# Spreading the loads of later token tiles and of output weights over the chunks of a fused attention and FFN kernel

## The chip, the cores and the metric

The kernel runs on one core of a Trainium2 chip. Its time is the device time of one execution in microseconds (us); each kernel was run several times, and the median is quoted. Three kinds of engine matter here: TensorE (PE in the profile; 8298 matmuls in the kernel before) multiplies matrices, VectorE (DVE, 1272 instructions) and ScalarE (ACT, 524) work on its results, and 16 DMA engines move data between memory and the on-chip buffer (212.49 MB). Nearly all transfers are issued by the sync engine (SP), in program order, from one queue (235,888 of 235,997 packets).

## The reference, cut to what matters

One token block of 2048 rows of 1024 goes through a layer norm with modulation, attention of 32 query heads over a window of 512 cached keys, an output projection with a gate, a second modulated layer norm and a SwiGLU FFN:

```python
h = _layernorm(x) * (1 + ca) + sa
x = x + ga * _A_ref(h, A_k_cache, A_v_cache, A_wq, A_wo)   # q = h @ wq; softmax(q k^T) v; @ wo
h = _layernorm(x) * (1 + cb) + sb
x = x + gb * _B_ref(h, B_w_gate, B_w_up, B_w_down)
```

No arithmetic changes. Only the moments change at which two kinds of load are issued.

## The kernel before

The 2048 rows are four chunks of four token tiles (128 rows, 256 KB each). A chunk's attention is a loop over 32 heads of about 3.3 us each (in the trace before 3.33 us in chunk 1, and from 3.23 us in chunk 3 to 3.69 us in chunk 0), followed by its output projection; after the four chunks come the four FFN chunks.

Query projections use a scheme with 7 products where 8 would be needed, so the query weights (1 MB for a group of four heads) also need weight sums. VectorE forms the sums during chunk 0, and the sums of each group are stored to memory (1 MB) and read back in later chunks (1 MB per group). The kernel keeps only two slots for groups of query weights, so a group's load waits until TensorE has finished with the group two before it:

```python
def load_wq(gi):                 # 2 x 512 KB, two slots
    ...
# in the head loop, i = running head
if i % 4 == 3 and i > 3:
    load_wq((i + 1) // 4 + 2)    # g computed first in the kernel
...
for k in range(4):               # chunk 0 and the groups up to HG + 1: the weight sums
    g = (i + 7 - k) // 4
    if i % 4 == (k + 1) % 4 and (3 if k < 2 else 2) <= g < HG + 2:
        weight_sums(g, DVE, V, (k,))
if i % 4 == 2 and i >= 6 and (i + 2) // 4 < HG + 2:
    store_sums((i + 2) // 4)
```

A group loaded at head 11 is thus read by VectorE at the end of head 13. The loads that the change moves stand in the same queue:

```python
if ch == 0:
    if h < 12:
        load_x(TPC + h)               # 12 token tiles at heads 0 to 11
    if h in (8, 10, 12):
        load_wo((h - 8) // 2)         # three output-weight tiles, 1 MB each

def oproj(ch, first, each):           # output projection of a chunk, 8 weight tiles through 3 slots
    ...
    for b_ in range(2, HG - 2):
        ...
        load_wo(ch * HG + b_ + 3)     # waits until TensorE is done with the slot
    for k in range(TPC * HALF):
        ...
    load_wo(ch * HG + HG + 1)         # the next chunk's second and third tile:
    load_wo(ch * HG + HG + 2)         # wait until the projection is over
```

Each head's result is also turned by a DMA transpose in the same queue (`oturn`), and layer norm tiles likewise (`ln_turn`).

The softmax here doesn't subtract the row's maximum and nothing guards it: scores larger than these inputs give would overflow.

## Time and profile before

| | before |
|---|---|
| median of 3 runs, us | 1269.97 (1269.24 to 1270.16) |
| span of the profiled run, us | 1266.0 |
| TensorE busy, us | 1246.4 (98%) |
| TensorE's waits of the table, 24 us to the end | 7.5 us |

The first view is the table of TensorE's waits from 24 us on (after the opening): who waited for whom, total us, number of waits, longest. L602 is the addition that finishes a query block, on VectorE.

```profile
PE ps L265 <- DVE arena L602: 4.0, 1, 4.0
PE ps L265 <- ACT arena L765: 1.2, 4, 0.3
PE ps L265 <- DMA arena<-wq_sums: 0.9, 1, 0.9
...
```

Two of the three have a load behind them: the 0.9 us openly, the 4.0 us through VectorE. Here is VectorE's and TensorE's timeline where the 4.0 us end (start us, us, engine, line, operation; in brackets the idle time before it and what ended it). L541 forms weight sums from the query weights.

```profile
81.61 0.69 DVE L541 TENSOR_TENSOR arena<-arena 128x1024 f16<-128x1024 bf16 x1 [4.06 <-DMA arena<-in_A_wq_dram]
82.22 0.42 DVE L602 TENSOR_TENSOR arena<-ps,arena 128x256 bf16<-128x256 f32 x1
...
82.70 1.57 PE L265 MATMUL ps<-arena 128*128 128x256 bf16 x9 [4.00 <-DVE arena L602]
```

In VectorE's order of work the addition stands behind the sums that wait for query weights, so they hold it back, and with it TensorE. The sync queue's timeline shows what stood before that load, which is the line L299 (L275 are token tiles, L503 output weights, L552 the store of sums, L676 and L371 transposes):

```profile
66.89 0.56 SPq L275 DMA_DIRECT2D arena<-in_A_x_dram  x1
67.50 0.42 SPq L503 DMA_DIRECT2D arena<-in_A_wo_dram  x1
68.03 1.82 SPq L676 DMA_TRANSPOSE arena<-arena  x1
69.89 0.57 SPq L552 DMA_DIRECT2D wq_sums<-arena  x1
70.51 0.44 SPq L275 DMA_DIRECT2D arena<-in_A_x_dram  x1
71.04 1.29 SPq L676 DMA_TRANSPOSE arena<-arena  x1
72.43 1.16 SPq L299 DMA_DIRECT2D arena<-in_A_wq_dram  x2
73.64 1.44 SPq L503 DMA_DIRECT2D arena<-in_A_wo_dram  x1
```

Issued at 72.43 us, used at 81.61 us. Last, stretches of 2 us after the wait: length, busy time of each engine with its number of instructions (TensorE, TensorE's weight loads, VectorE, ScalarE, GpSimd), the granted TensorE clock (1.00 is full), the DMA engines' share and GB/s.

```profile
80.00:82.00 2.00, 0.00 (x0) 0.00 (x0) 0.39 (x1) 0.00 (x0) 0.00 (x0) 0.93 1.09 370
82.00:84.00 2.00, 1.30 (x9) 1.05 (x10) 0.80 (x3) 1.24 (x2) 0.00 (x0) 0.50 1.07 357
84.00:86.00 2.00, 2.00 (x18) 1.81 (x17) 0.73 (x3) 0.06 (x1) 0.00 (x0) 0.50 1.74 275
86.00:88.00 2.00, 2.00 (x9) 1.11 (x8) 1.73 (x4) 0.38 (x1) 0.00 (x0) 0.50 0.96 107
88.00:90.00 2.00, 2.00 (x24) 1.50 (x22) 0.46 (x2) 1.94 (x2) 0.00 (x0) 0.87 0.89 323
```

In two of them TensorE counts as fully busy with the clock granted at half. Its matmuls of 129 columns start 108 ns apart in that time, and 57 ns apart from 89 us on. This loss is in nobody's wait.

### The profile page before, as it was taken

To read this page: it belongs to the slowest core of one execution; us is meant where nothing else is said; L and a number is where in the kernel's file an instruction comes from. 1 tells how busy PE (TensorE), PEld (TensorE's weight loads), DVE (VectorE), ACT (ScalarE), POOL (GpSimd) and SP (SyncE) were. 2 spreads that over 40 slices of the span, in tenths; PEclk is the share of its full clock that TensorE was granted. 3 is DMA by queue.
4 is the path that set the end of the run, shared out by engine and by line. 5 is a ranking of instruction groups with operands and counts; after the bars stand their busy time and mean duration, and the time that the engine had idled before them with its cause. 6 is when DMAs were issued, how large, how long until landed. Compare 5 with 4: busy or idle time off the path is not lost.

```text
span 1266.0 us, 20347 instructions
## 1 busy us (share of the span) xinstructions
PE 1246.4 (98%) x8298; PEld 711.2 (56%) x8298; DVE 613.5 (48%) x1272; ACT 379.2 (30%) x524; POOL 20.0 (2%) x41
## 2 busy tenths in 40 slices
PE   7989999999999999999999999999999999999999
PEld 4667646787457774588744444444444444444444
DVE  4968507886068770476504553245422643234321
ACT  4657404675036660267600111011100111011100
POOL 1000000000000000000000000000000000000000
PEclk9989999999999999999999999999999999999999
DMA  9997747996569874579257974037520655024200
GB/s 305 278 304 183 229 135 233 282 226 195 166 176 272 215 193 149 171 207 245 46 188 240 324 216 133 25 83 191 167 75 25 158 167 173 18 84 133 67 9 25
DMA packets 235997, 212.49 MB, mean 168 GB/s; under 512 B 106880, under 2 KB 206080, under 8 KB 232064
## 3 DMA queue, kind: packets, MB, share of 16 engines
q1 hardware_dynamic: 235888, 211.19, 59.0%
q8 instruction: 65, 1.06, 0.4%
q14 instruction: 28, 0.23, 0.1%
q10 hardware_dynamic: 16, 0.00, 0.0%
HBM read 174.07 MB, written 12.58 MB: 147 GB/s over the span
## 4 chain that ended last, share of the span: by engine, by line
PE 94%; DMA 2%; SPq 1%; DVE 1%; issue 1%; ACT 0%; DVEq 0%
PE ps L265 94%; DMA arena<-wq_sums 1%; DMA arena<-in_w_mod_dram 1%; DMA arena<-in_A_wq_dram 1%; SPq L284 1%; SPq L676 0%; DVE arena L670 0%; DVE arena L602 0%; DVE arena L748 0%; ACT arena L765 0%; DMA arena<-arena 0%; DVE arena L636 0%; SPq L275 0%; DVE arena L669 0%; DVE arena L541 0%
## 5 line engine op out<-in xcount | busy, mean ns | idle before, releaser
L265 PE MATMUL ps<-arena 128*128 128x512 bf16 (+4 forms) x8249 | 1243.1, 313 | 13.3 <-DMA arena<-in_w_mod_dram 4.3
L265 PEld LDWEIGHTS ps<-arena 128*128 128x128 bf16 (+1 forms) x8249 | 708.0, 98 | 547.8 <-issue 10.9
L653 ACT ACTIVATE arena<-ps 128x1024 bf16<-128x1024 f32 x256 | 249.7, 1022 | 40.3 <-PE ps L265 37.3
L977 ACT ACTIVATE arena<-ps 128x512 bf16<-128x512 f32 x112 | 66.9, 597 | 518.0 <-PE ps L265 518.0
L680 DVE TENSOR_TENSOR arena<-ps,arena 128x512 bf16<-128x512 f32 (+1 forms) x65 | 44.4, 684 | 338.9 <-PE ps L265 338.9
L978 DVE SCALAR_TENSOR_TENSOR arena<-arena,ps 128x512 bf16<-128x512 bf16 x112 | 77.0, 687 | 138.9 <-ACT arena L977 138.9
L596 ACT ACTIVATE arena<-ps 128x256 f32<-128x256 f32 x134 | 51.3, 383 | 258.6 <-PE ps L265 254.0
L980 DVE SCALAR_TENSOR_TENSOR arena<-arena,ps 128x512 bf16<-128x512 bf16 x112 | 77.1, 688 | 53.9 <-PE ps L265 53.8
L670 DVE TENSOR_TENSOR arena<-ps,arena 128x512 bf16<-128x512 f32 x128 | 88.5, 692 | 4.7 <-DMA arena<-arena 0.2
L602 DVE TENSOR_TENSOR arena<-ps,arena 128x256 bf16<-128x256 f32 x180 | 75.7, 421 | 11.8 <-PE ps L265 7.0
L669 DVE RECIPROCAL arena<-ps 128x4 f32<-128x4 f32 x128 | 23.1, 181 | 44.1 <-PE ps L265 43.4
L748 DVE SCALAR_TENSOR_TENSOR arena<-arena 128x512 f32<-128x512 bf16 x56 | 41.6, 743 | 0.1
L354 DVE BATCH_NORM_STATS2 arena<-arena 128x6 f32<-128x512 bf16 x60 | 41.2, 686 | 0.1
L541 DVE TENSOR_TENSOR arena<-arena 128x1024 f16<-128x1024 bf16 (+1 forms) x48 | 32.4, 683 | 4.2 <-DMA arena<-in_A_wq_dram 4.1
L361 POOL TENSOR_TENSOR arena<-arena 128x1 f32<-128x1 f32 x30 | 17.5, 583 | 991.7 <-DVE arena L359 989.2
L636 DVE CAST arena<-ps 128x256 bf16<-128x256 f32 x60 | 25.2, 420 | 11.4 <-PE ps L265 10.2
L682 DVE TENSOR_TENSOR arena<-arena 128x512 bf16<-128x512 bf16 (+1 forms) x65 | 27.4, 421 | 2.2
L598 DVE COPY arena<-ps 128x256 f32<-128x256 f32 x46 | 19.4, 422 | 14.6 <-PE ps L265 14.6
L375 DVE TENSOR_SCALAR arena<-arena 128x512 bf16<-128x512 bf16 x56 | 20.4, 408 | 0.0
L365 DVE TENSOR_SCALAR arena<-arena 128x1024 bf16<-128x1024 bf16 x32 | 17.3, 542 | 5.7 <-DMA arena<-arena 5.3
L269 PE MATMUL ps<-arena 128*128 128x128 bf16 (+1 forms) x49 | 4.9, 262 | 3.7 <-DVE arena L345 3.7
L358 DVE BATCH_NORM_AGGREGATE arena<-arena 128x2 f32<-128x12 f32 x30 | 6.3, 209 | 1.0
(43 smaller groups left out, 51.3 us busy)
## 6 DMA issues: line engine op xcount, KB each, us to landing
arena<-in_A_wq_dram SPq DMA_DIRECT2D x64, 512.0 KB, 4.7
arena<-in_A_wo_dram SPq DMA_DIRECT2D x32, 1024.0 KB, 5.3
arena<-in_B_w_gate_dram SPq DMA_DIRECT2D x28, 1024.0 KB, 5.4
arena<-in_B_w_up_dram SPq DMA_DIRECT2D x28, 1024.0 KB, 7.5
arena<-wq_sums SPq DMA_DIRECT2D x22, 1024.0 KB, 6.8
arena<-in_w_mod_dram SPq DMA_DIRECT2D x8, 1024.0 KB, 8.5
wq_sums<-arena SPq DMA_DIRECT2D x8, 1024.0 KB, 4.9
arena<-in_B_w_down_dram SPq DMA_DIRECT2D x4, 1792.0 KB, 11.1
```

The lines of the kernel that those rows point to most:

```text
L265: T.op(PE, lambda: TE.matmul(out_ap, lhsT, rhs, start=start, stop=stop, skip_group_check=loose), reads=reads, writes=bb)
L354: T.op(DVE, lambda: V.bn_stats(st_sb[i][:, 6 * hf:6 * hf + 6], x_sb[:, t, 512 * hf:512 * hf + 512]), reads=[BX[t]], writes=[B_st[i]])
L541: T.op(st, lambda: e.tensor_tensor(dst, x, y, op), reads=reads, writes=[dst_b])
L596: T.op(ACT, lambda: A.activation(sn[k], bank(QBK, 256), AF.Copy), writes=PB[QBK] + [B_sn[k]])
L602: T.op(DVE, lambda: V.tensor_tensor(dst, bank(XBK, 256, off), sn[k], ALU.add), reads=[B_sn[k]], writes=PB[XBK] + [B_q[i % NQ]])
L653: T.op(ACT, lambda: A.activation(ex[i % NEX][:, kt:kt + 2, :], bank(SCB[kt], 1024).rearrange("p (a b) -> p a b", a=2), AF.Exp, scale=att_s ...
L670: T.op(DVE, lambda: V.tensor_tensor(o_sb[i % NOS].rearrange("p (a b) -> p a b", a=TPC), num, rl_bc, ALU.mult), reads=[B_rl], writes=both + ...
L680: T.op(DVE, lambda: V.tensor_tensor(rt[s][:, 0:n], ps_ap, gate[:, lo:lo + n], ALU.mult), reads=[gate_b], writes=bb + [B_rt[s]])
L748: T.op(DVE, lambda: V.scalar_tensor_tensor(acc, ms[:, kc, :], sc[:, kc:kc + 1], acc, op0=ALU.mult, op1=ALU.add), reads=[B_ms, B_sc, B_acc] ...
L977: T.op(ACT, lambda: A.activation(th[e], bank(gb_), AF.Tanh, scale=0.5), writes=PB[gb_] + [B_th[e]])
L978: T.op(DVE, lambda: V.scalar_tensor_tensor(out=t1[e], in0=th[e], scalar=1.0, in1=bank(gb_), op0=ALU.add, op1=ALU.mult), reads=[B_th[e]], w ...
L980: T.op(DVE, lambda: V.scalar_tensor_tensor(out=gu[:, ft, :], in0=t1[e], scalar=0.5, in1=bank(ub_), op0=ALU.mult, op1=ALU.mult), reads=[B_t ...
```

## The change

The intent is to load each tile shortly ahead of its use. The token tiles of chunk 2 go to later heads of chunk 0, those of chunk 3 to chunk 1. The first output-weight tile of chunk 0 is loaded at head 13, and the second and third tile of every chunk at heads 17 and 22 of that chunk instead of at the end of the chunk before.

```diff
@@ in oproj, at its end
-                load_wo(ch * HG + HG + 1)
-                load_wo(ch * HG + HG + 2)
@@ in the head loop
                 if ch == 0:
-                    if h < 12:
+                    if h < TPC:
                         load_x(TPC + h)
-                    if h in (8, 10, 12):
-                        load_wo((h - 8) // 2)
+                    elif h in (19, 21, 24, 26):
+                        load_x(2 * TPC + (19, 21, 24, 26).index(h))
+                    elif h == 13:
+                        load_wo(0)
+                elif ch == 1 and h % 4 == 1 and h < 4 * TPC:
+                    load_x(3 * TPC + h // 4)
+                if h in (17, 22):
+                    load_wo(ch * HG + (17, 22).index(h) + 1)
```

## The prediction

> **What bounds it now.** TensorE: the page has it busy 1246.4 of 1266.0 us (98%), and the chain of waits is 94% one line of matmuls. The table of TensorE waits adds up to about 16 us, some 9 of them in the opening (before 24 us). So moving loads alone cannot reach 2% (25 us).
>
> **Where loads reach the critical path.**
>
> 1. Early in chunk 0. Between 44 and 74 us the timeline shows eight token tiles (256 KB each) and three output-weight tiles (1 MB each) issued among query weights, stores of weight sums and transposes. From 58 to 84 us the DMA view shows the engines full at 322 GB/s. Query weights issued at 72.43 us land near 81.6 us, in about 9 us (median 4.7). VectorE waits 4.06 us for them (its only such wait), and TensorE behind it 4.00 us (78.7 to 82.7 us).
> 2. The clock after it. Stretches of 2 us show the granted clock at 0.50 from 82 to 88 us, 0.87 in the next, then 1.00. Estimate from the busy times there: 5.3 us at half and 2.0 us at 0.87 lose 2.9 us. [...]
> 3. The boundary of chunks 1 and 2. During the output projection output-weight loads hold the queue, waiting for their buffers (eight issues over 48.7 us); the last go out at about 364 us. The load of weight sums follows at 369.19 us and needs 10.7 us (median 6.8). TensorE waits 0.93 us at 379 us.
>
> **What the change does.** No arithmetic and no bytes change. Token tiles of chunks 2 and 3 (2 MB) leave the burst, and so do the output-weight tiles (3 MB; the first returns at head 13, after the critical query weights). The query weights should land in about 5 us, near 77.5 us, just when VectorE gets to them. The 4.0 us wait and[...] the 2.9 us of half clock go. At each chunk's end two output-weight loads no longer stand before the next chunk's transposes and sums: the 0.9 us goes too.
>
> **What it adds.** Per chunk 2 MB of output weights at heads 17 and 22, and token tiles near heads 19 to 26 of chunk 0 and 1 to 13 of chunk 1. The engines move 200 to 320 GB/s there. In chunk 0 query weights have only about 5 us between issue and use, so the load at head 23, behind 1 MB of output weights and 1 MB of stored sums, could wait up to a microsecond. Later chunks have about 13 us. I allow 0.4 us.
>
> **Sum.** 4.0 + 2.9 + 0.9 - 0.4 = 7.4 us: 1269.97 - 7.4 = 1262.5 us. Range 1259.5 to 1266.
>
> **What would show it.** VectorE's wait on query weights below 1 us; no half clock after 30 us; the wait on weight sums near 379 us gone; DMA share from 58 to 84 us below 1; TensorE's busy time lower by about 3 us, its idle by about 5; FFN and opening unchanged.
>
> **What would make it wrong.** Query weights still queuing behind the 1 MB store of sums[...] (1268 to 1270 us); new waits at heads 17 to 27 of chunk 0; or VectorE, 98% busy from 45 to 58 us, being the next limit, so that TensorE only waits elsewhere.
>
> Chances: faster by over 2% 0.01, within 2% 0.98, slower 0.01.

Behind the 2.9 us stood the one trace before, with 4.00 us of idle and then a granted clock of 0.50; that the half clock would go with the wait was the estimate. The 1268 to 1270 us are the time with the wait and the half clock still there. The other figures without a source next to them come from the same trace: 203 GB/s from 97 to 123 us and 302 GB/s from 203 to 255 us for the stretches that take the moved loads, and four heads of 3.3 us for the 13 us of later chunks.

## The result, and the profile after

| | before | after |
|---|---|---|
| median, us | 1269.61 (4 runs) | 1260.46 (4 runs) |
| span of the profiled run, us | 1266.0 | 1257.6 |
| TensorE busy, us | 1246.4 | 1243.1 |

The ratio of the times is 0.9931 (95% interval 0.9914 to 0.9949), so about 8.8 us less. A ratio here is the mean time of one kernel's fast runs over that of the other's of the same rounds, so not quite the ratio of the medians in the table. In a later repetition it was 0.9938 (0.9926 to 0.9951).

TensorE's waits from 24 us on, after the change:

```profile
PE ps L265 <- ACT arena L763: 1.2, 4, 0.3
PE ps L265 <- DVE arena L636: 0.9, 3, 0.4
...
```

No load is among them any more, neither directly nor through L602. The same operations on VectorE as shown before:

```profile
77.26 0.68 DVE L541 TENSOR_TENSOR arena<-arena 128x1024 f16<-128x1024 bf16 x1
77.86 0.42 DVE L602 TENSOR_TENSOR arena<-ps,arena 128x256 bf16<-128x256 f32 x1
```

And the sync queue, from the same store of sums to the first output weights:

```profile
65.10 0.59 SPq L552 DMA_DIRECT2D wq_sums<-arena  x1
67.32 1.26 SPq L676 DMA_TRANSPOSE arena<-arena  x1
68.69 1.08 SPq L299 DMA_DIRECT2D arena<-in_A_wq_dram  x2
69.82 1.90 SPq L371 DMA_TRANSPOSE arena<-arena  x1
71.80 1.77 SPq L676 DMA_TRANSPOSE arena<-arena  x1
73.63 0.57 SPq L503 DMA_DIRECT2D arena<-in_A_wo_dram  x1
```

The query weights are issued 3.7 us earlier (68.69 against 72.43 us), though TensorE is at the same point of its work to within 0.2 us, and their two halves land in a median of 5.2 us, where they took 8.1 us before. All of them have landed at 74.9 us instead of 81.5 us. So the burst had cost twice: of these 6.6 us, 3.7 are a queue that had come to this load late, and the rest a transfer that then took longer. The clock stays whole:

```profile
82.00:84.00 2.00, 2.00 (x27) 1.75 (x25) 1.48 (x5) 1.29 (x3) 0.00 (x0) 1.00 0.97 335
84.00:86.00 2.00, 2.00 (x23) 1.51 (x21) 1.15 (x3) 1.95 (x4) 0.00 (x0) 1.00 1.34 132
```

The 8.4 us between the two spans can be laid out along TensorE's timeline, because the same pieces of work begin at known times. The opening gave 0.2 us, by chance: the difference is there at 24 us, and the first load that the change moves was issued at 44.73 us. From the piece that starts at 63.28 us (before) and 63.08 us (after) to the one that starts at 103.73 and 96.55 us, the old kernel took 40.45 us and the new one 33.47 us: 6.98 us, of which 4.00 are the wait and the other 2.98 the half clock. From 133.29 to 439.42 us it took 306.13 us, and from 126.09 to 431.04 us 304.95 us: 1.18 us, of which 0.93 is the wait for the stored sums at the boundary of chunks 1 and 2. After that nothing differs (826.6 us in both).

### The profile page after: what moved, and what is told of

Its sections match the earlier page's. It is cut to its first block, busy times and chain, and to the rows that moved or that the text cites. A ratio compares the mean times of both kernels' runs of the same rounds, so it can differ in the third digit from the quotient of the medians.

```text
span 1257.6 us, 20341 instructions
## 1 busy us (share of the span) xinstructions
PE 1243.1 (99%) x8298; PEld 709.7 (56%) x8298; DVE 612.6 (49%) x1272; ACT 379.0 (30%) x524; POOL 20.0 (2%) x41
## 4 chain that ended last, share of the span: by engine, by line
PE 96%; DVE 1%; SPq 1%; DMA 1%; issue 1%; ACT 0%
PE ps L265 96%; DMA arena<-in_w_mod_dram 1%; SPq L284 1%; DVE arena L670 0%; DVE arena L746 0%; ACT arena L763 0%; DVE arena L602 0%; DMA arena<-arena 0%; DVE arena L636 0%; DVE arena L669 0%; SPq L275 0%; SPq L299 0%; PE ps L269 0%; DVE arena L354 0%; DVE arena L541 0%
## 5 line engine op out<-in xcount | busy, mean ns | idle before, releaser
L602 DVE TENSOR_TENSOR arena<-ps,arena 128x256 bf16<-128x256 f32 x180 | 75.5, 420 | 11.0 <-PE ps L265 6.3
```

The source lines that it names most:

```text
L602: T.op(DVE, lambda: V.tensor_tensor(dst, bank(XBK, 256, off), sn[k], ALU.add), reads=[B_sn[k]], writes=PB[XBK] + [B_q[i % NQ]])
```

## The experiments

Every kernel below gave correct results. Waits and half clock are read from one profiled execution each, so they are samples; the ratio is against the kernel before in the same rounds.

| kernel | ratio, 95% interval | VectorE's waits for query weights, us | half clock, us |
|---|---|---|---|
| token tiles only | 0.9994 (0.9978 to 1.0011) | 1.74 and 2.20 | 3.41 |
| output weights of chunk 0 only | 0.9973 (0.9961 to 0.9985) | 1.96 | 0 (no record) |
| both of these | 0.9956 (0.9942 to 0.9970) | 0 | 0 (no record) |
| chunk ends only | 0.9995 (0.9983 to 1.0008) | 4.72 | 3.41 |
| the whole change, again | 0.9938 (0.9926 to 0.9951) | 0 | 0 |
| token tiles in two loads | 1.0001 (0.9988 to 1.0015) | 4.59 | 6.83 |
| other order | 1.0040 (1.0018 to 1.0061) | 8.8, in two waits | 6.83 |
| burst on ScalarE's queue | 1.0038 (1.0023 to 1.0053) | 8.00 and 0.69 | 10.24 |

The half clock is the sum over stretches of 0.25 us of the share by which the granted clock fell short, times two, from 24 us on; the kernel before has 6.83 us of it. The two traces marked "no record" hold no record of the clock, and the profile then shows 1.00. Their matmuls settle it: those of 129 columns start 57 ns apart after each wait, as they do in the kernel before where its granted clock is 1.00.

The mean granted clock of each execution is on record too, and shows how far one trace is typical (with no record it reads 1.000). Of 27 executions of the kernel before in these rounds none reached 1.000 (0.996 to 0.999); with the whole change eight of nine did, with both parts three of five, with the output weights of chunk 0 only two of five. The profiled execution of that last kernel is its fastest, and better than its usual one.

The first question is which part of the change does the work. The first theory was a threshold: 2 MB taken out ahead of the critical load should do. The rival was that the parts share the gain by their bytes.

**Token tiles only.** The token tiles move as in the change, the output weights stay.

```diff
-                    if h < 12:
+                    if h < TPC:
                         load_x(TPC + h)
+                    elif h in (19, 21, 24, 26): load_x(...)      # and chunk 3's tiles in chunk 1, as in the change
```

> Only the token tiles of chunks 2 and 3 move; output weights stay as before. Theory A (a backlog with a threshold: any 2 MB taken out of the queue ahead of the critical query weights is worth some 6 us of transfer, more than the 4.06 us that VectorE waits): wait of VectorE on query weights below 0.5 us, no half clock, about 7 us gained (near 1262.5 us), the boundary wait of 0.9 us stays. Theory B (the gain is shared out by bytes, 2 of 5 MB): a wait of about 2.4 us stays, no half clock, about 4.5 us gained.

The "some 6 us" are an estimate: 2 MB at the 322 GB/s of the kernel before (58 to 84 us) take 6.5 us.

The median was 1267.57 us against 1268.57, with a wide spread (1263.04 to 1270.84). The threshold theory was wrong. The wait at head 13 shrank from 4.06 to 1.74 us, and a second one appeared one group later:

```profile
94.54 0.69 DVE L541 TENSOR_TENSOR arena<-arena 128x1024 f16<-128x1024 bf16 x1 [2.20 <-DMA arena<-in_A_wq_dram]
```

TensorE then stood idle for 2.13 us, and the clock went to half for one stretch of 3.41 us. The rival's 2.4 us was nearer for the one wait, but it had no second wait and no half clock, and its 4.5 us did not come. The critical query weights were issued early here, but their halves still took 8.2 and 8.3 us to land:

```profile
69.16 2.43 SPq L299 DMA_DIRECT2D arena<-in_A_wq_dram  x2
```

**Output weights of chunk 0 only.** They go to heads 13, 17 and 22; the token tiles stay.

```diff
-                    if h in (8, 10, 12):
-                        load_wo((h - 8) // 2)
+                    if h in (13, 17, 22):
+                        load_wo((13, 17, 22).index(h))
```

> Only the three output-weight tiles of chunk 0 move (to heads 13, 17, 22); token tiles stay as before, and so do the loads at the chunk ends. Theory A (threshold): 2 MB less ahead of the critical query weights, so a wait below 0.5 us, no half clock, about 7 us gained (near 1262.5 us), boundary wait stays. Theory B (by bytes, 3 of 5 MB): a wait of about 1.6 us stays, about 5 us gained.

1264.45 us, a gain of 0.27% (3.4 us) where the theories had 7 and 5 us. At head 13 there was no wait, but a wait of 1.96 us came at head 17, for the next group. So both theories failed on the place: about half of the delay had gone, the rest had moved on to the next group's load. The critical query weights were issued late here, but their halves landed in 4.6 and 5.5 us:

```profile
71.59 1.09 SPq L299 DMA_DIRECT2D arena<-in_A_wq_dram  x2
```

So the two costs of the burst come apart in these two traces. Without the token tiles the load is issued at 69.16 us, close to the 68.69 us of the whole change, and its transfer stays slow. Without the output weights it is issued at 71.59 us, close to the 72.43 us of the kernel before, and its transfer is quick.

**Both.** These two together, with the loads at the chunk ends left as before.

```diff
+ token tiles as in the change, output weights of chunk 0 at heads 13, 17, 22
  load_wo(ch * HG + HG + 1) and load_wo(ch * HG + HG + 2) stay at the end of oproj
```

> Both halves of the chunk 0 part together (token tiles and the three output-weight tiles move), the loads at the chunk ends as before. If the two halves alone each left a lag that only moves to the next group, and the boundary is a matter of its own: VectorE never waits for query weights, no half clock, about 7 us gained against before, and TensorE's wait for the sums near 372 us (up to 1 us) stays. If the parts simply added up (0.8 and 3.4 us by the means of the earlier runs): about 4 us gained and a wait of some 2 us left.

1262.55 us against 1268.78. No wait for query weights, no half clock. The ratios of the single parts give 0.06% and 0.27%, together the parts give 0.44%; the intervals are too wide to say whether that is more than the sum. In the traces it is hardly more: over the stretch from 63 to 104 us of the kernel before (the same weight loads of TensorE), token tiles alone took 1.6 us less, output weights alone 4.9 us and both 7.0 us. What both together do, and neither alone, is to leave no wait for query weights. But TensorE now waited for stored sums twice, once in a place where the kernel before has no wait:

```profile
251.41 68.80 PE L265 MATMUL ps<-arena 128*128 128x256 f16 x611 [1.62 <-DMA arena<-wq_sums]
...
374.67 25.60 PE L265 MATMUL ps<-arena 128*128 128x256 f16 x267 [0.85 <-DMA arena<-wq_sums]
```

The new one is in chunk 1, where chunk 3's token tiles have gone. Token tiles only shows it too, at 256 us (1.29 us). After the whole change it is not there.

**Chunk ends only.** The burst stays.

```diff
-                load_wo(ch * HG + HG + 1)        # end of oproj
-                load_wo(ch * HG + HG + 2)
+                elif h in (17, 22):              # chunks 1 to 3; chunk 0 as before
+                    load_wo(ch * HG + (17, 22).index(h) + 1)
```

> The burst of chunk 0 stays as before; only the last two output-weight loads of a chunk's end go to heads 17 and 22 of the next chunk. My theory: TensorE's wait on the weight sums near 379 us goes, the 4.0 us wait near 79 us and the half clock stay, 1.0 to 1.2 us gained (near 1268.6 us; within the spread of runs, so the trace decides). Rival (the sums are late for another reason, such as the modulation load in front of them): the 0.9 us wait stays.

1267.4 us against 1268.57, a difference that the interval does not tell from none. The trace does: no wait for stored sums is left, and the wait near 79 us (4.6 us in this trace) and a half clock are. So the part at the chunk ends is worth its 0.9 us alone, and more in company: with it the 1.62 us wait of the kernel above goes as well. With the whole change the sync queue issues that load of sums at 240.48 us; in the kernel above it came to it at 245.06 us, with TensorE at the same point of its work to within 0.2 us. So there the queue was late again, and the loads at the chunk ends were what had made it late. In time, the whole change is 0.9938 and both chunk 0 parts are 0.9956 in the same rounds.

**The whole change, again,** on the chip of the run of both:

> The change as a whole, again, on the same chip as the run of both chunk 0 halves. Expected: 8 to 9 us gained against before as measured the first time, about 1 us better than the chunk 0 halves without the boundary, no wait for loads after 24 us.

1260.97 us, and no wait for a load after 24 us: the first result, repeated.

The second question is what in the burst makes the load late: the number of issues, the order in the queue, or the work for the DMA engines.

**Token tiles in two loads.** The eight tiles of chunks 2 and 3 go as two loads of 1 MB.

```diff
-                    if h < 12:
+                    if h < TPC:
                         load_x(TPC + h)
+                    if h in (6, 10):
+                        load_x4(8 if h == 6 else 12)   # four tiles in one transfer
```

> The kernel before, but the eight token tiles of the burst go as two loads of 1 MB (at heads 6 and 10) instead of eight of 256 KB: six issues fewer, same bytes. If it is the number of issues that makes the queue late: wait for the query weights of head 11 below 2 us. If it is what the engines have to move: the wait stays at 3.5 to 5 us with the half clock behind it, and the time within 2 us of before.

1268.68 us against 1268.78; the wait was 4.59 us. With six issues fewer the query weights were issued at 72.45 us, as late as before, and took 8.4 and 9.3 us to land. The number of issues is not it.

**Other order.** Three token tiles and one output-weight tile go behind the critical query weights.

```diff
-                    if h < 12:
+                    if h < 9:
                         load_x(TPC + h)
-                    if h in (8, 10, 12):
-                        load_wo((h - 8) // 2)
+                    if h == 8:  load_wo(0)
+                    if h == 12: load_wo(1); load_x(13); load_x(14); load_x(15); load_wo(2)
```

> The kernel before, but three token tiles (13, 14, 15) and the second output-weight tile go into the queue after the query weights of head 11 instead of before them; the bytes of the stretch are the same. Theory C (the queue runs late and in order: what stands ahead of the query weights delays them, and the lag moves on to the next group): no wait above 0.5 us for the query weights of head 11, but a wait of 2 to 4 us for those of head 15; total gain under 4 us. Rival (the engines share their bandwidth among everything in flight, so order is nothing): the wait at the query weights of head 11 stays above 2 us.

1273.5 us, 0.4% slower than before. The wait at head 13 fell to 1.05 us, twice the most that the theory allowed but well under the rival's 2 us; the next one became far larger than expected, and TensorE stood still for 7.65 us:

```profile
103.16 7.12 PE L265 MATMUL ps<-arena 128*128 128x256 bf16 x58 [7.65 <-DVE arena L602]
```

Order decided which load was late here (1.05 us of wait for the first, 7.65 us behind the next), as the theory said; the size was wrong (2 to 4 us expected), and the time rose where a gain of up to 4 us was expected. Putting the same bytes elsewhere within the busy stretch did not help.

**Burst on ScalarE's queue.** The eight token tiles and three output-weight tiles are issued by ScalarE at the same heads.

```diff
-  SP.dma_start(x_sb[:, t, :], ...)      SP.dma_start(wo[n], ...)
+  A.dma_start(x_sb[:, t, :], ...)       A.dma_start(wo[n], ...)      # t >= 8, n < 3
```

> The kernel before, but the eight token tiles and three output-weight tiles of the burst are issued by ScalarE on its own queue, at the same heads; bytes and time of issue are about the same. Theory C (the lag of the one queue): the sync queue issues the query weights of head 11 near 69 us, as after the change, and they land in time: wait below 1 us, no half clock, 1262 to 1265 us. Rival (bytes in the stretch are too many for the engines, whatever queue): they land near 80 us or later, wait above 2 us, 1266 to 1270 us.

1272.81 us, 0.4% slower than before. This is against what I had expected, and worse than the rival's 1266 to 1270 us. The query weights of the group before the critical one, issued at 57.76 us, became available only at 72.39 us, and VectorE waited 8.00 us for them:

```profile
72.39 0.69 DVE L541 TENSOR_TENSOR arena<-arena 128x1024 f16<-128x1024 bf16 x1 [8.00 <-DMA arena<-in_A_wq_dram]
```

The sync queue lost its burst and was no better for it. The two queues had the same 16 DMA engines to share: from 60 to 75 us the packets of the one with the burst took 53.9% of the engines' time, and those of the sync queue 51.7%. The halves of this group took 11.2 and 13.9 us to land, where in the kernel before the same group took 4.8 and 5.7 us, and VectorE had not waited for it. I read the runs so: what the whole change gives is time, because it takes work away from a stretch in which the engines have no room (share 1.13 from 58 to 84 us before, 1.00 after). What makes the sync queue itself late is not shown: it is not the number of issues, and I did not measure what the transposes take.

The third question is the half clock: is it TensorE's idle time that brings it, or the full DMA engines?

**Fillers in the wait of the kernel before.** 16 matmuls of 512 columns with no use are put where TensorE waits, into a bank that the next product overwrites.

```diff
+                if i == 14:
+                    for _ in range(16):
+                        mm(bank(OBK), kT[:, 0, :], kT[:, 0:4, :]..., True, True, [B_kT[0]], PB[OBK])
```

> The kernel before with 16 filler matmuls (512 wide, about 3.45 us together) where TensorE waits for the late query weights; they write a bank that the next product overwrites from the start. My theory (idle TensorE halves the clock): VectorE's wait of about 4 us stays, TensorE's idle falls below 1 us, the clock stays at 1.00, and 2.9 us are gained (near 1266.7 us). Rival (the clock falls for another reason, such as the full DMA engines in that stretch): half clock of about 6 us stays, nothing gained.

The 3.45 us are an estimate from the kernel before, where matmuls of 512 columns start 216 ns apart at a granted clock of 1.00.

Inconclusive. In this trace the query weights came later than in the kernel before: VectorE waited 6.62 us for them, so TensorE was idle for 3.1 us after the fillers, and the clock fell for 3.41 us. The time was 1269.59 us against 1268.57, so nothing was gained. Why the load came later is open. I had relied on a wait of a fixed length; it isn't one.

**A wait of chosen length in the kernel after,** without any late load: six idle VectorE operations of 0.69 us.

```diff
+                    if i == 13 and k == 0:
+                        for _ in range(6):
+                            T.op(DVE, lambda: V.bn_stats(rt[0]..., x_sb[:, 4, 0:512]), ...)
```

> The kernel after with six idle VectorE operations (0.69 us each, 4.1 us) put where VectorE waited for the query weights in the kernel before; no load is late. Theory (an idle TensorE halves the clock, DMA has no part in it): TensorE idle near 4 us at 78 to 82 us, then half clock[...], 1.7 to 3.4 us lost on top of the 4.1: 1266 to 1268 us. Rival (full DMA engines did it): clock stays at 1.00, 1264.5 us.

> The same with 16 filler matmuls (3.45 us) in the wait. Theory: TensorE idle below 1 us, clock 1.00, so about 4.1 us lost and not more: 1264 to 1265 us, 2 to 3 us below the run without filler. Rival (filler is no help, the clock falls all the same or fillers delay the products): the same as without, or slower.

The 0.69 us are those of the same operation in the kernel before (686 ns on 128x512). The 1.7 to 3.4 us are an estimate: half of the half clock measured by then, 3.41 us (token tiles only) and 6.83 us (before).

The medians were 1265.77 us without fillers and 1264.37 us with them. These are the waits of TensorE, and below each a stretch before and one after their end, first without and then with fillers:

```profile
82.37 20.64 PE L265 MATMUL ps<-arena 128*128 128x256 bf16 x188 [4.08 <-DVE arena L602]
80.00:82.00 2.00, 0.00 (x0) 0.00 (x0) 1.97 (x4) 0.00 (x0) 0.00 (x0) 0.76 1.18 384
84.00:86.00 2.00, 2.00 (x17) 1.69 (x15) 0.57 (x2) 0.00 (x0) 0.00 (x0) 0.50 0.00 0
```

```profile
83.96 17.99 PE L265 MATMUL ps<-arena 128*128 128x256 bf16 x188 [0.62 <-DVE arena L602]
80.00:82.00 2.00, 2.00 (x11) 0.91 (x10) 1.90 (x4) 0.07 (x1) 0.00 (x0) 1.00 1.42 208
84.00:86.00 2.00, 2.00 (x27) 1.89 (x28) 0.65 (x3) 1.35 (x3) 0.00 (x0) 1.00 0.93 393
```

The DMA engines are full when the clock falls in the run without fillers (share 1.18 from 80 to 82 us). With fillers they are as full in those two microseconds (1.42), TensorE is idle for only 0.62 us, and the clock stays whole. So full DMA engines alone did not bring the half clock; and without fillers it stays at half while they do nothing at all (share 0.00 from 84 to 86 us). From the piece that starts at 62.86 us without fillers, and at 64.45 us with them, to the one at 103.23 and 102.17 us it is 40.37 us without and 37.72 us with fillers: 2.65 us saved (the medians differ by less, 1.4 us; in this pair of traces the run with fillers also lost 1.6 us in its opening, where its clock was at half from 24.80 to 28.21 us; what brought that is not shown). The kernel after takes 33.47 us there. So an idle of 4.1 us cost 6.9 us here: 4.1 for itself and 2.8 for the clock. That is what the kernel before paid (6.98 us).

## Why the prediction was right

The prediction was 1262.5 us with a range of 1259.5 to 1266; the measurement was 1260.46 us. Point by point:

- "TensorE bounds the kernel, so moving loads alone cannot reach 2%." Right: the gain was 0.69%.
- "The 4.0 us wait goes." Right, and the runs of the parts show that neither half of the chunk 0 part does it alone. The reasoning was only half right. I had put the lateness down to a transfer of 9 us instead of 5. In the trace after, 3.7 of the 6.6 us come from an earlier issue: the queue itself had been behind, which I had not foreseen. The forecast "land near 77.5 us, just when VectorE gets to them" was therefore too cautious; they had landed at 74.9 us. To that extent it was luck: with the shorter transfer alone, the second half (issued at 73.06 us before, 5.6 us of transfer after) would have landed near 78.7 us, an estimate, and VectorE, which came to it at 77.55 us, would still have waited about 1.1 us.
- "The 2.9 us of half clock go." Right: 2.98 us in the traces, and the chosen wait with and without fillers shows that it was TensorE's idle time that brought the loss. How much idle it takes stays open: with token tiles only, a wait of 2.13 us had a half clock of 3.41 us behind it. After the change the longest wait of TensorE from 24 us on is 0.4 us.
- "The boundary wait of 0.9 us goes." Right, 0.93 us; the stretch around it became 1.18 us shorter. I have no account of the other 0.25 us.
- "I allow 0.4 us for new waits." Mis-sized: VectorE has no wait for query weights at all in both traces of the change, and TensorE none for a load after 24 us. Without the part at the chunk ends the allowance would have been too small: 1.62 us in chunk 1, which I had held to be free ("later chunks have about 13 us"). The change avoids this only because it also clears the chunk's start.
- "DMA share from 58 to 84 us below 1." Wrong: it fell from 1.13 to 1.00 with 253 instead of 322 GB/s. The engines are as good as full after the change too; but the load that counts is no longer late.
- "TensorE's busy time lower by 3 us, idle by 5." Right: 3.3 us, and idle from 19.6 to 14.5 us (span less busy time).

The sum of the terms in the traces is 0.2 (opening) + 4.00 + 2.98 + 1.18 = 8.4 us, the difference of the spans; the prediction had 4.0 + 2.9 + 0.9 - 0.4 = 7.4 us. The gap comes from the allowance (0.4), from the boundary (0.3) and from the opening (0.2).

## What to carry to other kernels

Before you judge a load by its transfer time, compare its issue time with that of a kernel without the burst: here a queue that had fallen behind issued the load that counted 3.7 us late, and removing a part of the burst, changing the order or using another queue moved all or part of the wait to another load. A wait of TensorE can cost more than its length: here 4.1 us of it cost 6.9 us, because the granted clock fell to 0.50 after it; count both. Parts of a schedule change can depend on each other, as the loads at the chunk ends did here, so test the parts together before you drop one that shows nothing alone.
